# Where an identity matrix is made: GpSimd's select, or a running sum and a block transpose on VectorE

## The chip, the core and the metric

One core of a Trainium2 chip runs one program from the first load to the last store. The metric is the device time of that program in microseconds (us), lower is better. TensorE multiplies matrices, VectorE (DVE in the profile) and ScalarE (ACT) work element by element, GpSimd (POOL) makes constants, reduces over partitions and issues indirect transfers, and SyncE (SP) issues most of the loads.

## The reference

Linear attention, a mixture of experts over its output, and a gated feed-forward stage. Only the attention's beginning matters here:

```python
def phi(x):
    proj = np.einsum('bhsd,df->bhsf', x, w_phi)
    proj = proj - np.max(np.abs(proj), axis=-1, keepdims=True)
    return np.concatenate([np.exp(proj), np.exp(-proj)], axis=-1)
q_p, k_p = (phi(q), phi(k))
kv = np.einsum('bhsf,bhsd->bhfd', k_p, v)
z = np.sum(k_p, axis=2)
num = np.einsum('bhsf,bhfd->bhsd', q_p, kv)
den = np.einsum('bhsf,bhf->bhs', q_p, z)[..., None] + 1e-06
```

There are 4 batches of 8 heads, 576 tokens and 64 dimensions, and 128 features. The result, 2304 tokens of 512, goes through 8 experts (each token through one) and then through a feed-forward stage of width 768.

## The kernel before

The attention is cut into steps: on the k side a head quad of a 256-token unit (`k_T` transposes the keys, `k_proj` projects them, `k_acc` accumulates keys times values and the sums of the keys, `k_fin` ends a batch), on the q side a half batch and a head pair (`q_T` transposes, `q_front` projects and reduces over partitions on GpSimd, `q_sub`, `q_exp`, `q_num`, `q_den` and so on). Python generators, interleaved by `merge`, write the order of TensorE, SP, GpSimd and VectorE out by hand: each engine takes its instructions in that order. ScalarE is left to the scheduler. The first instructions of TensorE are eleven products that nothing uses (line 151), then `k_T(0)`, `k_T(1)`, `k_proj(0, 0)`, `k_proj(0, 1)` (twelve products), then the first query transposes `q_T(0, 0)`, `k_proj(1, 0)` and the first accumulation, `k_acc`.

Every transpose on TensorE is a product with the identity `ident`, a 128x128 tile in float32. `make_identity` (line 1154) makes it on GpSimd: a memset to zero and a select that writes ones where row and column are equal. It is called ahead of the block in which the order is written out. `Routing.__init__` (lines 573 to 601) then makes the constants of the routing on GpSimd (four iotas, several memsets, a select), and the attention makes its own (`ones`, two `zp`, `enp`, lines 157 to 165) after them in GpSimd's order. The routing's constants are used when the attention is over; `ones` in the sums of the keys. GpSimd's first work after the constants is the partition reduction of line 332.

Loads: SP issues the first key unit in two halves, its values, the first query block, and the next unit of keys and values (lines 91 and 108); ScalarE's queue issues the two copies of the projection weights into `w2` (lines 138 and 140). VectorE clears `wkH` and `wkL` (line 148; the unused products read `wkL`) and, when the weights are there, splits them (lines 152 to 156).

Of the kernel before, what the change touches and what calls it, by code (L numbers as in the profile page):

```python
# [18 lines left out]

#: steps of a batch's k side, of the first q work over two a unit, and of a batch's q side  # L20
PACE = 47, 9, 35


def merge(*streams):
    """Interleave streams of work; each is a list of (generator, its expected steps), and stages keep pace."""
    live = [[list(st), 0, 0] for st in streams]

    def progress(s):
        return s[1] + min(s[2] / s[0][0][1], 0.999)

    while live:
        for s in sorted(live, key=progress):
            try:
                if next(s[0][0][0]) == "blocked":
                    continue
                s[2] += 1
            except StopIteration:
                s[0].pop(0)
                s[1] += 1
                s[2] = 0  # L40
                if not s[0]:
                    live.remove(s)
            break
        else:
            raise RuntimeError("all streams blocked")


def rsqrt(nc, pool, out, in_, shape, nm):
    """out = in_ ** -0.5 by Newton steps from the exponent trick; yields between them."""
    g = pool.tile(shape, F32, tag=f"rs_g{nm}", name=f"rs_g{nm}")  # L50
    t = pool.tile(shape, F32, tag=f"rs_t{nm}", name=f"rs_t{nm}")
    i = pool.tile(shape, I32, tag=f"rs_i{nm}", name=f"rs_i{nm}")
    nc.vector.tensor_scalar(g, in_, 1e-30, None, op0=ALU.max)
    nc.vector.tensor_scalar(i, g.bitcast(I32), 1, None, op0=ALU.logical_shift_right)
    nc.vector.tensor_scalar(out.bitcast(I32), i, -1, 0x5F3759DF, op0=ALU.mult, op1=ALU.add)
    for _ in range(3):
        nc.vector.tensor_tensor(t, out, out, op=ALU.mult)
        nc.vector.tensor_tensor(t, t, g, op=ALU.mult)
        nc.vector.tensor_scalar(t, t, -0.5, 1.5, op0=ALU.mult, op1=ALU.add)
        nc.vector.tensor_tensor(out, out, t, op=ALU.mult)  # L60
        yield


def attention(tc, q, k, v, w_phi, expert_emb, tau, x_d, lraw, ssq, ident, io, late, rt):
# [11 lines left out]
    with ExitStack() as ctx:  # L76
# [6 lines left out]

        # ---- loads
        kt, vt, qt = {}, {}, {}
# [27 lines left out]

        # steps on the k side: a head quad of a 256-token unit, or the rests of two batches
        steps, pcs, loads = [], [], []
# [48 lines left out]
        enp = cp.tile([P, NP_, 32], F32, tag="enp", name="enp")  # L164
        nc.gpsimd.memset(enp, 0.0)

        def prep_experts():
# [27 lines left out]

        # ---- k side
        kT, kp, kvs, acc = {}, {}, {}, {}
# [100 lines left out]

        # ---- q side: unit u = (half batch, head pair)
        stk, pq, mq, ex, ot, dn = {}, {}, {}, {}, {}, {}  # L300
# [84 lines left out]
        def x_log(ts):  # L385
            """logits of a few tiles; and one over their denominators"""
            n = len(ts)
# [35 lines left out]

        # ---- order of work
        load_kv(2)
# [54 lines left out]
        def q_ahead(u):  # L480
            """front work that precedes back unit u - LEAD"""
            m, p = divmod(u, NP_)
            if u < NU:
                q_front(u)
            if u - 2 >= 0 and u - 2 < NU:
                q_sub(u - 2)
# [72 lines left out]

#: moves a double's exponent, in its upper word read as float32, to float32's bias  # L560
REBIAS = 2.0 ** -112
#: added and taken away, it rounds to a whole number
ROUND = 1.5 * 2.0 ** 23


#: products that keep the tensor engine's clock up where it waits: for the routing (four places), for the first loads
WARM = 8, 22, 8, 2, 11


class Routing:  # L570
    """Sort the tokens by expert: into blocks of 128 slots, each of one expert, and densely."""

    def __init__(self, tc, gp, rp, NT, E, NB):
        self.tc, self.nc, self.gp, self.rp = tc, tc.nc, gp, rp
        self.NT, self.E, self.NB = NT, E, NB
        nc, P = tc.nc, 128

# [28 lines left out]
    def one_hots(self, pool, r, nm, groups):  # L606
        """rows r (1 to 128) of the tiles' tokens as one-hot matrices, a group of tiles at a time"""
        P = 128
# [9 lines left out]
    def warm(self, bank, n):  # L618
        """products that nothing uses"""
        if n:  # L620
# [4 lines left out]
    def argmax(self, lraw, t0, t1):  # L625
        """one-hot expert of tiles t0 to t1 - 1; the first of equal logits wins"""
        V, P, E = self.nc.vector, 128, self.E
# [11 lines left out]
    def blocks(self, bank):  # L639
        """slot of every token, token of every slot, expert of every block; yields where the vector engine waits"""  # L640
        nc, gp, rp, P, NT, E, NB = self.nc, self.gp, self.rp, 128, self.NT, self.E, self.NB
# [11 lines left out]
        yield  # L653
        # slots of every expert's blocks, one block at least
        nb = t_([P, E], "nb")
# [9 lines left out]
        V.tensor_tensor(ohb, ohb.bitcast(F32), self.tid.unsqueeze(2).to_broadcast(full), op=ALU.mult)  # L665
        # token of every slot
        ps3 = bank("rt_tok")
        for group in self.one_hots(rp, rf, "R", (6, 6, 6)):
# [4 lines left out]
            yield  # L673
        # expert of every block
        eb = t_([1, NB, E], "eb")
# [5 lines left out]
        V.tensor_copy(self.s2t, ps3[:, 0:NB])  # L681
        # places of the experts in the dense order
        self.before = self.tmp(gp, [P, E], "before")
# [13 lines left out]
    def places(self, rp, gp, first, before, nm):  # L697
        """place of every token, from 0, less (P - 1) / 2; its expert's places start at `first`"""
        V, P, E, NT = self.nc.vector, 128, self.E, self.NT
# [10 lines left out]
    def rows(self, rp, pos, nm):  # L710
        """of places less (P - 1) / 2: row in the tile, from 1, and first place of the tile"""
        V, P, NT = self.nc.vector, 128, self.NT
# [6 lines left out]
    def dense(self, rp, bank, gate):  # L719
        """token, slot and gate of every place in the dense order"""  # L720
        nc, gp, P, NT, E = self.nc, self.gp, 128, self.NT, self.E
# [42 lines left out]
def gates(tc, rp, lraw, ssq, gate):  # L764
    """softmax weight of the chosen expert, token by token"""
    nc = tc.nc
# [22 lines left out]
class Experts:  # L789
    """Raw expert weights on chip: four chunks of [128, 2048], expert 0's first, reloaded when the expert changes."""  # L790

# [4 lines left out]
    def alloc(self, pool):  # L796
        """in the space of the attention's inputs, which are used up"""
        self.raw = [pool.tile([128, 2048], F32, tag=tag, name=f"raw{i}") for i, tag in enumerate(("kv", "kv", "q", "q"))]
        for i in range(4):
            self.load(i, slice(0, 1))  # L800
# [11 lines left out]
class Moe:  # L812
    """y = relu(x @ w1) @ w2, block by block of 128 slots"""

# [8 lines left out]
    def run(self, j0, j1, before=None, during=None):  # L823
        """blocks j0 to j1 - 1"""
        nc, sp, pp, wp, ex, ident = self.nc, self.sp, self.pp, self.wp, self.ex, self.ident
# [131 lines left out]
class Moe2:  # L957
    """h = max(y @ w1, y @ w2, y @ w3), out = h @ w_out, over thirds of the tokens"""

# [39 lines left out]
    def rebias(self, n):  # L999
        """double words: the exponent as float32 has it, still three bits too low"""  # L1000
        if n < 2 * self.NF and self.wide:
# [4 lines left out]
    def cut(self, n):  # L1006
        """a chunk of weights in float32: double words are cut to 24 bits; yields between steps"""
        if n >= 2 * self.NF:
# [30 lines left out]
    def gather(self, t):  # L1039
        """a tile of the dense order; its slots lie in the first t + 8 blocks"""  # L1040
        if t >= self.NT:
# [23 lines left out]
    def run(self, n0):  # L1065
        """all but the first third's y and the first n0 parts of the weights, which are there"""
        tc, nc, P, NF, NK, DM, G, TG, NT = self.tc, self.nc, self.P, self.NF, self.NK, self.DM, self.G, self.TG, self.NT
# [72 lines left out]
def tile_kernel(ctx, tc, q, k, v, w_phi, expert_emb, tau, w1, w2, m2_w1, m2_w2, m2_w3, m2_w_out, out):  # L1140
# [12 lines left out]
    ident = gp.tile([P, P], F32, tag="ident", name="ident")  # L1153
    make_identity(nc, ident)
    lraw = gp.tile([P, NT, E], F32, tag="lraw", name="lraw")
# [4 lines left out]
    with ExitStack() as rctx:  # L1160
        rp = rctx.enter_context(tc.tile_pool(name="rt", bufs=1))
        with tc.manual_schedule(engines={ET.PE, ET.SP, ET.Pool, ET.DVE}):
            rt = Routing(tc, gp, rp, NT, E, NB)
            attention(tc, q, k, v, w_phi, expert_emb, tau, x_d, lraw, ssq, ident, ew, lambda: ex.alloc(ew), rt)
    with tc.manual_schedule():
        pre = ctx.enter_context(tc.tile_pool(name="m2pre", bufs=1))
        m2 = Moe2(tc, pre, m2_w1, m2_w2, m2_w3, m2_w_out, NTOK, NB, ys, rt, out, ident)
        with mctx:
# [15 lines left out]
            def weights():  # L1184
                """the first parts of the next stage's weights"""
                m2.load_w(0)
# [73 lines left out]
```

## Time and profile before

| | us |
|---|---|
| median of 3 runs | 854.7 |
| the runs | 856.23, 852.54, 854.70 |
| span of the profiled execution | 855.8 |
| TensorE busy | 826.1 (97%) |
| VectorE busy | 548.4 (64%) |
| ScalarE busy | 493.2 (58%) |
| GpSimd busy | 162.0 (19%) |

The page gives no other time of the profiled execution than its span, from its first instruction to its last. Busy times are of that one execution. A matmul's end is modelled, so a busy TensorE is not one at its peak.

### The profile page before, as it was taken

Reading aid. Unit: us, or ns where it says so; the run is one execution under the profiler, and the core shown is the slowest. Engines: PE = TensorE matmul, PEld = TensorE weight load, DVE = VectorE, ACT = ScalarE, POOL = GpSimd, SP = SyncE. Lnnn points to the kernel's source line nnn. Section 1 sums busy time; section 2 is a strip of 40 time slices with the busy share of each in tenths; the row PEclk is TensorE's granted clock in tenths of the full one; section 3 lists DMA queues with packets and bytes.
Section 4 is the critical chain, followed back from the end, with each engine's and each line's share of the span. In section 5 each row is a group of like instructions: output and inputs, shape, how many; then the busy total and the mean of one; then the engine's idle time right before and its main releaser. Section 6 shows DMA issues by size and latency. Waiting matters only on the chain. (4 is left out here: it accounts for less than half of the span.)

```text
span 855.8 us, 13159 instructions
## 1 busy us (share of the span) xinstructions
PE 826.1 (97%) x5049; PEld 671.4 (78%) x5049; DVE 548.4 (64%) x705; ACT 493.2 (58%) x680; POOL 162.0 (19%) x116
## 2 busy tenths in 40 slices
PE   5989999999988999999999999999999999999996
PEld 4555565555567888888888888899989999899995
DVE  4886777767587999999889898788412222122210
ACT  3788868878647888888888796444221111211111
POOL 1234323233313122101051212000031001200001
PEclk9999999999998999999999999999999999999998
DMA  8331333310622435743644644344021000200001
GB/s 182 78 78 28 103 75 103 102 39 19 229 72 89 167 117 182 282 182 118 234 168 144 218 171 169 118 155 141 13 79 58 1 1 24 75 13 1 1 21 53
DMA packets 59649, 87.73 MB, mean 103 GB/s; under 512 B 7160, under 2 KB 37496, under 8 KB 59584
## 3 DMA queue, kind: packets, MB, share of 16 engines
q1 hardware_dynamic: 51376, 65.03, 23.8%
q0 software_dynamic: 4880, 15.99, 5.7%
q10 hardware_dynamic: 3328, 5.83, 1.8%
q8 instruction: 41, 0.67, 0.3%
q14 instruction: 24, 0.20, 0.1%
HBM read 129.58 MB, written 15.99 MB: 170 GB/s over the span
## 5 line engine op out<-in xcount | busy, mean ns | idle before, releaser
L864 DVE TENSOR_TENSOR wL<-raw,wH 128x2048 fp32r<-128x2048 f32 x88 | 199.6, 2287 | 18.3 <-ACT wH L863 17.9
L863 ACT CAST wH<-raw 128x2048 fp32r<-128x2048 f32 x88 | 167.6, 1915 | 30.8 <-PE ph L890 13.7
L1091 PE MATMUL ps<-yH,m2WH 128*128 128x384 f32 x432 | 146.1, 338 | 1.3 <-ACTq L1227 1.3
L1091 PE MATMUL ps<-yH,m2WL 128*128 128x384 f32 x432 | 146.0, 338 | 0.0
L1091 PE MATMUL ps<-yL,m2WH 128*128 128x384 f32 x432 | 146.0, 338 | 0.0
L332 POOL PARTITION_ALL_REDUCE mq<-pq x32 | 68.9, 2159 | 143.7 <-DVE pq L336 94.1
L1099 ACT CAST h2H<-mm 128x384 fp32r<-128x384 f32 x36 | 18.5, 513 | 118.4 <-DVE mm L1096 118.4
L1091 PEld LDWEIGHTS ps<-yH,m2WH 128*128 128x128 f32 x432 | 81.1, 188 | 1.8 <-ACTq L1227 1.7
L1091 PEld LDWEIGHTS ps<-yL,m2WH 128*128 128x128 f32 x432 | 81.1, 188 | 0.1
L1091 PEld LDWEIGHTS ps<-yH,m2WL 128*128 128x128 f32 x432 | 81.1, 188 | 0.0
L834 POOL DMA_INDIRECT xs<-x_d,s2t x22 | 43.7, 1988 | 155.5 <-PE psxT L873 93.6
L1045 POOL DMA_INDIRECT yg<-ys,c2s x18 | 26.2, 1454 | 245.4 <-PE psyT L1060 220.6
L922 PE MATMUL py<-wH,hH 128*128 128x512 f32 x176 | 70.4, 400 | 0.4 <-ACT hH L908 0.4
L922 PE MATMUL py<-wH,hL 128*128 128x512 f32 x176 | 69.1, 392 | 0.0
L922 PE MATMUL py<-wL,hH 128*128 128x512 f32 x176 | 68.7, 390 | 0.0
L1095 DVE TENSOR_TENSOR mm<-mm,ps 128x384 f32<-128x384 f32 x36 | 19.9, 552 | 76.2 <-PE ps L1091 76.2
L321 DVE TENSOR_TENSOR st<-psqT,st 64x288 fp32r<-64x288 f32 x64 | 44.7, 698 | 36.6 <-ACT st L317 34.6
L890 PE MATMUL ph<-wH,xH 128*128 128x512 f32 x176 | 57.4, 407 | 0.7 <-ACT xH L876 0.7
L890 PE MATMUL ph<-wL,xH 128*128 128x512 f32 x176 | 55.4, 396 | 0.0
L890 PE MATMUL ph<-wH,xL 128*128 128x512 f32 x176 | 55.2, 395 | 0.0
L1096 DVE TENSOR_TENSOR mm<-mm,ps 128x384 f32<-128x384 f32 x36 | 19.9, 554 | 45.6 <-PE ps L1091 45.6
L1113 ACT ACTIVATE ot<-pso,gatec 128x512 f32<-128x512 f32 x18 | 12.4, 688 | 60.3 <-PE pso L1111 33.0
(222 smaller groups left out, 1594.8 us busy)
## 6 DMA issues: line engine op xcount, KB each, us to landing
raw<-in_moe_w_dram SPq DMA_DIRECT2D x88, 1024.0 KB
wr<-in_moe_w_dram SPq DMA_DIRECT2D x18, 512.0 KB
ys<-y ACTq DMA_DIRECT2D x22, 256.0 KB
q<-in_q_dram SPq DMA_DIRECT2D x8, 576.0 KB
x_d<-x SPq DMA_DIRECT2D x18, 256.0 KB
kv<-in_v_dram SPq DMA_DIRECT2D x8, 512.0 KB
kv<-in_k_dram SPq DMA_DIRECT2D x7, 512.0 KB
wr<-in_moe_w_out_dram SPq DMA_DIRECT2D x6, 512.0 KB
```

Of the source, the lines that this page charges most:

```text
L321: nc.vector.tensor_tensor(st[o, :, :, 2 * rp + j], psv[x], st[x, :, :, 2 * rp + j].bitcast(F32), op=ALU.subtract)
L332: nc.gpsimd.partition_all_reduce(mx.rearrange("p a b -> p (a b)"), d.rearrange("p a b -> p (a b)"), P, ReduceOp.absmax)
L834: nc.gpsimd.indirect_dma_start(out=d, out_offset=None, in_=self.x_d, in_offset=bass.IndirectOffsetOnAxis(ap=self.s2t[:, j:j + 1], axis=0))
L863: nc.scalar.copy(wH, ex.raw[i])
L864: nc.vector.tensor_tensor(wL, ex.raw[i], wH.bitcast(F32), op=ALU.subtract)
L890: nc.tensor.matmul(ph[:, n * 512:(n + 1) * 512], a[:, cs], w[:, c * DF + n * 512:c * DF + (n + 1) * 512], start=(kc == 0 and f == 0), stop ...
L922: nc.tensor.matmul(py, a[:, cs], w[:, ws], start=(fc == 0 and q == 0), stop=(fc == 7 and q == 2))
L1045: self.nc.gpsimd.indirect_dma_start(out=d, out_offset=None, in_=self.ys[0:rows, :], in_offset=bass.IndirectOffsetOnAxis(ap=self.rt.c2s[:, ...
L1091: nc.tensor.matmul(ps, w[:, c], y[:, k], start=(k == 0 and q == 0), stop=(k == NK - 1 and q == 2))
L1095: nc.vector.tensor_tensor(m, m, pss[1], op=ALU.max)
L1096: nc.vector.tensor_tensor(m, m, pss[2], op=ALU.max)
L1099: nc.scalar.copy(hH[:, f], m)
```

## The change

`make_identity` goes. A new function makes the identity on VectorE: a row of ones is summed up, so that each of 32 columns holds its number from 1 to 32 in all partitions; the 32x32 blocks of that are transposed, so that each partition holds its own number within its group of 32; and for each of the four groups the columns are compared with that number, which writes ones and zeros into the diagonal blocks of a cleared `ident`. It is called as the first thing in the block whose order is written out, ahead of `Routing` and of the attention. The scratch tile's pool closes at the function's end. `Routing`'s constants move from its constructor into a method `prep`, which the attention calls after `enp`: GpSimd now has the attention's constants first and the routing's after them. The rest of the diff takes comments away.

```diff
-from concourse.masks import make_identity
...
+def identity(tc, out):
+
+    V = tc.nc.vector
+    with tc.tile_pool(name="idn", bufs=1) as pool:
+        a = pool.tile([128, 3, 32], F32, tag="idn", name="idn")
+        V.memset(a[:, 0], 1.0)
+        V.memset(out, 0.0)
+        V.tensor_tensor_scan(a[:, 1], a[:, 0], a[:, 0], 0.0, op0=ALU.mult, op1=ALU.add)
+        V.transpose(a[:, 2], a[:, 1])
+        for i in range(0, 128, 32):
+            V.tensor_scalar(out[i:i + 32, i:i + 32], a[i:i + 32, 1], a[i:i + 32, 2, 0:1], None, op0=ALU.is_equal)
+
...
         enp = cp.tile([P, NP_, 32], F32, tag="enp", name="enp")
         nc.gpsimd.memset(enp, 0.0)
+        rt.prep()
...
         self.NT, self.E, self.NB = NT, E, NB
+
+    def prep(self):
+        tc, gp, NT, E, NB = self.tc, self.gp, self.NT, self.E, self.NB
         nc, P = tc.nc, 128
...
     ident = gp.tile([P, P], F32, tag="ident", name="ident")
-    make_identity(nc, ident)
...
         with tc.manual_schedule(engines={ET.PE, ET.SP, ET.Pool, ET.DVE}):
+            identity(tc, ident)
             rt = Routing(tc, gp, rp, NT, E, NB)
```

## Rows read from the trace of the kernel before

**Rows 1.** The page: busy tenths of TensorE and its granted clock, 40 slices.

```profile
PE   5989999999988999999999999999999999999996
...
PEclk9999999999998999999999999999999999999998
```

**Rows 2.** TensorE's waits over the span: us in total, times, longest us.

```profile
PE pskT L210 <- POOL ident masks.py:199: 5.8, 1, 5.8
```

**Rows 3.** Timeline to 25 us: start us, us, engine, line, operation, tiles [idle before <-releaser].

```profile
0.82 0.56 ACTq L138 DMA_DIRECT2D w<-in_w_phi_dram  x1
...
1.22 0.27 DVE L148 MEMSET wkL<- 128x256 f32 x1
...
1.54 2.71 PE L151 MATMUL warm<-wkL 128*128 128x256 f32 x11 [1.54 <-DVE wkL L148]
...
5.28 0.23 DVE L152 CAST wqH<-w 128x128 fp32r<-128x128 f32 x1 [3.79 <-DMA w<-in_w_phi_dram]
...
6.46 0.23 DVE L156 CAST wkL<-wqL 64x128 fp32r<-64x128 f32 x1
...
9.62 0.14 POOL L580 IOTA we<- 128x8 f32 x1 [8.59 <-issue]
9.72 0.28 POOL masks.py:199 TENSOR_SCALAR_AFFINE_SELECT ident<-ident 128x128 f32<-128x128 f32 x1
...
10.06 1.97 PE L210 MATMUL pskT<-ident,kv 128*128 128x128 f32 x8 [5.80 <-POOL ident masks.py:199]
...
11.85 0.58 PE L227 MATMUL pskp<-wkH,kH 128*128 128x256 f32 x1
...
12.47 0.20 POOL L165 MEMSET enp<- 128x128 f32 x1
...
12.57 0.58 PE L227 MATMUL pskp<-wkH,kL 128*128 128x256 f32 x1
...
14.87 0.54 PE L312 MATMUL psqT<-ident,q 72*128 72x72 f32 x4
...
16.80 0.63 ACT L234 ACTIVATE kp<-pk 128x512 f32<-128x512 f32 x1
...
18.01 0.65 PE L260 MATMUL kv<-kp,kv 128*64 128x256 f32 x4 [1.85 <-ACT kp L235]
```

**Rows 4.** Pool configurations of lines 580 and 332: ns min/median/max, first and last start.

```profile
L580 POOLq MODIFY_POOL_CONFIG  x2: 8/8/8, 1.0 to 1.1; - x2
...
L332 POOLq MODIFY_POOL_CONFIG  x2: 11/11/11, 12.9 to 12.9; - x2
```

**Rows 5.** Stretches: busy us per engine, granted clock, DMA share, GB/s (last column).

```profile
0.00:9.00 9.00, 2.71 (x11) 2.42 (x11) 1.86 (x8) 1.28 (x1) 0.41 (x5) 1.00 0.78 193
9.00:11.40 2.40, 1.34 (x7) 1.35 (x8) 0.00 (x0) 0.19 (x1) 1.65 (x11) 1.00 1.21 192
11.40:13.90 2.50, 2.50 (x11) 2.06 (x11) 1.45 (x3) 0.98 (x2) 1.28 (x7) 1.00 1.18 227
```

**Rows 6.** Small VectorE operations by shape, count | busy us, mean ns | idle before.

```profile
L647 DVE TENSOR_TENSOR_SCAN inc<-d,oh 128x144 f32<-128x144 f32 x1 | 0.5, 457 | 0.0
...
L394 DVE TENSOR_SCALAR r<-psxd 128x24 f32<-128x24 f32 x2 | 0.4, 183 | 1.3 <-PE psxd L391 1.3
...
L659 DVE TENSOR_TENSOR_SCAN cb<-o,nb 128x8 f32<-128x8 f32 x1 | 0.2, 175 | 0.0
```

**Rows 7.** Two later stretches: length, busy us of PE, PEld, DVE, ACT, POOL, granted clock.

```profile
18.00:25.30 7.30, 7.29 (x36) 4.65 (x37) 5.46 (x9) 5.32 (x9) 0.00 (x0) 0.54 0.24 53
...
30.00:60.00 30.00, 26.85 (x223) 15.79 (x220) 28.68 (x58) 26.85 (x51) 11.86 (x6) 0.99 0.36 91
```

**Rows 8.** Timeline, 25 to 45 us: the first partition reduction, the next query transposes.

```profile
28.91 2.16 POOL L332 PARTITION_ALL_REDUCE mq<-pq  x1 [16.23 <-ACT pq L330]
...
29.43 0.42 PE L312 MATMUL psqT<-ident,q 72*128 72x72 f32 x4
```

## The prediction, made before the change was run

> **What bounds the kernel now.** I read the forty slices of the page first. TensorE is busy nearly everywhere except in the first slice, and no granted clock is far below full for a whole slice [rows 1]. So the change, which touches only constants made at the very start, can win time in that first slice or nowhere. Next comes the list of waits of TensorE over the whole run: its largest single wait is 5.8 us, and what ended it is the identity made on GpSimd [rows 2]. Third, the timeline of the first 20 us shows how that comes about. GpSimd's first iota starts at 9.62 and the select that writes the ones of `ident` at 9.72, after 8.59 us in which it waited for nothing that the profile lists [rows 3]. The rows of line 580 tell what lies there: a pool configuration is issued at 1.1 [rows 4]. I read the 8.5 us from 1.1 to 9.62 as the price of that configuration. TensorE, done with its unused warm products at 4.25, stands still until 10.06, then transposes keys, and everything behind it (copy on ScalarE, difference on VectorE, projection at 11.85, query transposes at 14.87, exponentials at 16.80, first accumulation at 18.01) hangs on that start [rows 3].
>
> [...]
>
> **The change, part by part.**
>
> *Removed from the path: identity behind the pool configuration.* The identity no longer needs GpSimd. With it ready, the first key transposes have to wait for the warm products and for the first key transfer, half of a 512 KB unit and the first thing in SP's queue. That whole unit and the two loads of the weights are 0.59 MB, reached at 3.1 us by the mean rate of the first 9 us [rows 5], so the transfer is not what they wait for.
>
> *Added: eight instructions on VectorE, ahead of the two clears and the warm products.* Two memsets: I take for each the 0.27 us of a 256 column one [rows 3], which is more than these 32 and 128 columns need. A running sum of 32 elements: 0.175 us with 8 and 0.457 with 144 elements [rows 6], so 0.23 in between. The block transpose has no row; its bounds are a 24 column operation (0.183) and that 144 element scan (0.457) [rows 6], and I take 0.23, nearer to the row of its own width. Four comparisons of 32x32: 0.183 each by the 24 column row [rows 6]; the six casts and differences from 5.28 to 6.69 [rows 3] start 0.235 apart on average though each works on at most 128 columns, so I take 0.235. Sum: 0.54 + 0.23 + 0.23 + 0.94 = 1.9 us, with ends of 1.4 (eight at 0.175) and 2.6 (the wide scan for scan and transpose, and 0.29 a comparison).
>
> [...]
>
> Queued behind these eight on VectorE are the clears of `wkH` and `wkL`; behind these, on TensorE, the eleven warm products, and behind them the key transposes. The products thus start at 1.54 + 1.9 = 3.4 and last 2.71, to 6.15 [rows 3]; ends 5.65 and 6.85. The first key transposes start there instead of at 10.06: 3.9 us earlier (3.2 to 4.4). The split weights are ready at 6.69 [rows 3], which is before the projection wants them (11.85 - 3.9 = 7.95), so the later clears cost nothing else.
>
> *What is late next: the queries.* TensorE takes its work in order, and after the twelve projections come the transposes of the first query block, at 14.87 now, at 10.95 with the shift. Their 576 KB transfer lies fourth in SP's queue. Up to its end the queues carry 256 + 256 + 512 + 576 KB from SP and 64 KB of weights, 1.70 MB. By the rates of the first stretches, 1.74 MB had moved by 9.0 us; with the next key unit 2.23 MB, reached at 11.5; with the next values too 2.75 MB, reached at 13.9 [rows 5]. The transfers share the DMA engines, so the query block lands between 8.9 and 13.9. I let it end with the unit behind it and add some tenths for the hand-over: 11.8, an estimate. Then its transposes start at 11.9 instead of 14.87, 3.0 us earlier, and ScalarE, which has the copies of these transposes ahead of the first exponentials (16.80) in its order, passes this shift on to the accumulation, 18.01 to 15.0 [rows 3]. So 0.9 of the 3.9 us is lost again, and it is also the cover for the identity: up to 0.9 us more on VectorE would cost nothing.
>
> *Moved: GpSimd's order.* `ones`, the two `zp` and `enp` now come before the iotas. All of GpSimd's constants together took from 9.62 to 12.67 [rows 3], so the moved ones end by 3.9 at the latest, and are ready long before the first sums use them. The iotas and the rest then follow behind the configuration, at 3.9 + 8.5 = 12.4 or earlier, and end by 15.5. Their users (routing, far behind) cost nothing. Behind them comes a second configuration, for the partition reduction, now issued at 12.9 [rows 4]; with another 8.5 us the engine would be ready at 24.0 at the latest. The first reduction is wanted at 28.91 now [rows 8], at 25.9 with the shift. So 1.9 us of cover remain at the least. The next query block, transposed at 29.43 now [rows 8], is issued behind the first key and value units as before and has been loaded by then.
>
> *A possible new wait.* The scratch tile of the identity lives in a pool that closes before the attention's constants are placed, so the first of these, `w2`, may get the same bytes. Then its two loads on ScalarE's queue, issued at once today, wait for the last comparison, at 0.94 + 1.9 = 2.85. From the issue of these loads to the use of the weights passed 5.28 - 0.82 = 4.5 us [rows 3]; then they would come at 7.3, be split by 8.7, and the differences of the keys, which VectorE does behind that, by 9.4; the products that need these start at 12.57 now [rows 3]. That is a shift of 3.2, about that of the queries. I count it at nothing, with ends of nothing and of the fourth case below.
>
> *Sum.* 5.8 us of waiting removed; 1.9 us given to VectorE's chain ahead of the warm products; 0.9 us given to the query transfer: 3.0 us gained. On the profiled execution's span of 855.8 that makes 852.8; this span lies 1.1 us above the median of the runs shown, 854.7, and from the median it makes 851.7.
>
> **The rivals.**
> *The shift is larger.* If the queries land at 8.9, the transposes pass without a wait and 3.9 us remain. The granted clock can add to that: the stretch from 18 to 25.3 ran at 0.54 with TensorE busy 7.29 of 7.3 us, while VectorE had 5.46 of work in it [rows 7]. With TensorE busy from 3.4 on without the long pause, the clock may be up there; VectorE then bounds the stretch, worth up to 1.8. Against it: TensorE still pauses for the queries and for the first exponentials (1.85 us before 18.01 [rows 3]), and after this pattern the clock fell. Time: 854.7 - 3.9 to 5.7, 849.0 to 850.8, say 850.0.
> *Another wait takes most of it.* The queries land with the next values at 13.9, or the weights come a microsecond or two later than above. Gain 0.9, time 853.8.
> *Slower: the weights fall behind SP's queue.* If `w2` waits for the scratch tile and its loads are then served only with the 2.75 MB that SP has queued, they land at 13.9; with 1.4 for the splits and 0.7 for the difference of the keys, the products that need it start at 16.1 instead of 12.57 [rows 3]: 3.5 us late, 858.2. It decides from a landing later than 10.4. Against it: today the loads, issued side by side with SP's, were used at 5.28, when less than half of that had moved.
> *The change does nothing:* not if the select leaves GpSimd; then the 5.8 us row must go.
>
> **How the numbers follow.** Forecast, gain of 2 to 4 us: 0.55. Larger shift: 0.22. Most of it lost: 0.17. Slower: 0.06. About 0.5% (4.3 us) is what a measurement of this kernel can tell from no change, so faster means below 850.4, slower above 859.0. Most of the larger shift lies below 850.4, with a little of the forecast's edge: faster 0.22. Of the slower case half may pass 859.0: slower 0.03. Same: 0.75. The range takes in the larger shift's middle and the lost gain: 849.2 to 855.0.
>
> **What would show it.** In the changed kernel's timeline: eight VectorE instructions ending near 2.8, warm products from 3.4, key transposes near 6.2 with no wait on GpSimd; TensorE then waiting for a DMA of `q`, the query transposes near 11.9, the first accumulation near 15.0, the first partition reduction near 26. I am wrong if `w2` is used later than 8, if the reduction's configuration is waited for, if the query transposes pass without a wait, or if the 3 us seen at 15 are no longer there at 60.

## The result, and the profile after

| | before | after |
|---|---|---|
| median time, us | 854.69 (852.54 to 856.23) | 859.13 (857.33 to 860.73) |
| ratio after/before, 95% | | 1.0057 [1.0046, 1.0069] |
| profiled execution: time, span, us | -, 855.8 | 857.33, 855.6 |
| mean granted clock of that execution | 0.987 | 0.985 |

The change made the kernel 4.4 us slower; 851.7 with a range to 855.0 had been forecast. The profiled executions don't show it: both spans are about 855.7. The time of the profiled execution after lies 1.7 us above its span. With as much around it, the one before (855.8) took about 857.5, more than any of its six timed runs. So the kernel before was profiled once more, as `e0_before_again`; that execution (853.56 us, span 851.8) lies 0.9 us below the median of its set, as the one after lies 1.8 below its own, and what follows is compared with it. One timed run of the experiments below (1021.92 us at a mean granted clock of 0.751, of `e3_order_only`) was in a slow state and is left out.

The page of the kernel after, busy tenths of TensorE and granted clock in 40 slices, beside [rows 1]:

```profile
PE   5899999999979999999999999999999999999996
...
PEclk8899999999998999999999999999999999999998
```

The first slice is no fuller than before, the second is emptier, and the clock dropped in both. The timeline of the kernel after, to 28 us (columns as in [rows 3]):

```profile
0.90 0.09 DVE L52 MEMSET idn<- 128x32 f32 x1 [0.90 <-PEq L1260]
...
1.04 0.20 DVE L54 TENSOR_TENSOR_SCAN idn<-idn 128x32 f32<-128x32 f32 x1
1.27 0.21 DVE L55 STREAM_TRANSPOSE idn<-idn 128x32 f32<-128x32 f32 x1
1.52 0.97 DVE L57 TENSOR_SCALAR ident<-idn 32x32 f32<-32x32 f32 x4
...
2.53 0.56 ACTq L150 DMA_DIRECT2D w<-in_w_phi_dram  x1
...
5.72 1.85 PE L223 MATMUL pskT<-ident,kv 128*128 128x128 f32 x8
...
10.91 0.23 DVE L164 CAST wqH<-w 128x128 fp32r<-128x128 f32 x1 [7.75 <-DMA w<-in_w_phi_dram]
...
11.98 0.55 PE L240 MATMUL pskp<-wkH,kH 128*128 128x256 f32 x1 [4.41 <-DVE wkH L168]
...
14.52 0.14 POOL L596 IOTA we<- 128x8 f32 x1 [10.79 <-issue]
...
18.71 0.65 PE L273 MATMUL kv<-kp,kv 128*64 128x256 f32 x4 [1.25 <-ACT kp L248]
...
27.44 2.16 POOL L345 PARTITION_ALL_REDUCE mq<-pq  x1 [11.25 <-ACT pq L343]
```

The wait for the identity is gone: the key transposes start at 5.72 instead of 10.06. But the load of the weights on ScalarE's queue is issued at 2.53 instead of 0.82, when the last comparison has ended, and the weights are used at 10.91 instead of 5.28. TensorE waits 4.41 us for them, and the first projection starts at 11.98 (11.85 before), the first accumulation at 18.71 (18.01). A second loss follows later. ScalarE, from 26 to 37 us, kernel after:

```profile
26.60 0.70 ACT L343 COPY pq<-psqf 128x288 f32<-128x288 f32 x2
29.52 0.63 ACT L247 ACTIVATE kp<-pk 128x512 f32<-128x512 f32 x1 [2.22 <-DVE pk L245]
30.06 0.61 ACT L248 ACTIVATE kp<-pk 128x512 f32<-128x512 f32 x1
30.78 0.63 ACT L247 ACTIVATE kp<-pk 128x512 f32<-128x512 f32 x1
31.32 0.61 ACT L248 ACTIVATE kp<-pk 128x512 f32<-128x512 f32 x1
31.84 1.33 ACT L330 CAST st<-psqT 64x288 fp32r<-64x288 f32 x2
33.19 0.58 ACT L226 CAST kH<-pskT 128x512 fp32r<-128x512 f32 x1
33.67 0.62 ACT L189 ACTIVATE esq_junk<-emb 8x512 f32<-8x512 f32 x1
```

And the same work of the kernel before, in `e0_before_again`:

```profile
26.21 0.70 ACT L330 COPY pq<-psqf 128x288 f32<-128x288 f32 x2
26.79 0.63 ACT L176 ACTIVATE esq_junk<-emb 8x512 f32<-8x512 f32 x1
...
27.70 1.38 ACT L317 CAST st<-psqT 64x288 fp32r<-64x288 f32 x2 [0.20 <-PE psqT L312]
29.13 0.63 ACT L234 ACTIVATE kp<-pk 128x512 f32<-128x512 f32 x1
29.67 0.61 ACT L235 ACTIVATE kp<-pk 128x512 f32<-128x512 f32 x1
30.31 0.58 ACT L213 CAST kH<-pskT 128x512 fp32r<-128x512 f32 x1
```

ScalarE does the same instructions in another order. Before, the square of `emb` and the two copies of the query transposes (`st`) come ahead of the exponentials (`kp`); after, they come behind four of them, and ScalarE stands 2.22 us for VectorE's `pk` (what the exponentials read: projections less their maxima) with those copies queued behind. VectorE, which wants `st` next, then stands too, in the kernel after:

```profile
33.20 1.34 DVE L334 TENSOR_TENSOR st<-psqT,st 64x288 fp32r<-64x288 f32 x2 [2.45 <-ACT st L330]
```

Stretch 30 to 33 us, columns as in [rows 7], first after, then `e0_before_again`:

```profile
30.00:33.00 3.00, 2.31 (x26) 0.84 (x24) 0.71 (x2) 2.88 (x6) 0.00 (x0) 1.00 0.21 55
```

```profile
30.00:33.00 3.00, 3.00 (x31) 1.53 (x30) 2.82 (x8) 2.98 (x7) 0.37 (x1) 1.00 0.23 58
```

VectorE did 0.71 us of work in these 3 us against 2.82. The diff doesn't touch ScalarE's program. The orders of TensorE, VectorE, GpSimd and SyncE are written out by hand in this kernel; ScalarE's is left to the scheduler. What it plans from, no run shows. Compared instruction by instruction, the two kernels' ScalarE orders differ in 25 places, all from the 22nd to the 72nd instruction.

### The profile page after: what moved, and what is told of

Its sections match the earlier page's. It is cut to its first block, busy times and chain, and to the rows that moved or that the text cites. A ratio compares the mean times of both kernels' runs of the same rounds, so it can differ in the third digit from the quotient of the medians.

```text
span 855.6 us, 13166 instructions
## 1 busy us (share of the span) xinstructions
PE 825.3 (96%) x5049; PEld 670.7 (78%) x5049; DVE 549.5 (64%) x713; ACT 492.8 (58%) x680; POOL 161.0 (19%) x114
## 5 line engine op out<-in xcount | busy, mean ns | idle before, releaser
L330 ACT CAST st<-psqT 64x288 fp32r<-64x288 f32 x64 | 43.6, 682 | 8.4 <-PE psqT L325 7.9
```

What stands on the lines that cost most here:

```text
L330: nc.scalar.copy(st[x, :, :, 2 * rp + j], psv[x])
```

## The experiments

The first theory had one cause: the scratch tile `idn` shares its bytes with `w2`, so the loads of the weights are held. The rival was the moved order on GpSimd; a third theory, ScalarE's order, was formed when the first had fallen. Each run's median is set beside that of the kernel before in the same set. A convenient clock within one execution is the row of the partition reductions on GpSimd (they recur 32 times): they show at which point a kernel falls behind.

**The kernel before, once more** (`e0_before_again`). No edit.

> The kernel before once more, as it is, for a second profile. The profile of before had a span of 855.8 us while its six timed runs have a median of 854.7; the six runs of the changed kernel lie 1.7 us above their spans. If a profile is one draw of a time that scatters with where TensorE's clock falls (clock theory), this one has its low-clock stretches elsewhere, up to 20 us apart, and a span that differs by 1 to 4 us, most likely near 853. If the start is a fixed cost (loads theory), the first accumulation starts at 18.0 again, the span is 855.8 again and the low clock lies at 18.5 to 25.4 again.

Measured: 854.47 against 854.5, 1.0004 [0.9989, 1.0018]; span 851.8. First, second and ninth reduction:

```profile
27.04 2.16 POOL L332 PARTITION_ALL_REDUCE mq<-pq  x1 [14.83 <-ACT pq L330]
32.63 2.14 POOL L332 PARTITION_ALL_REDUCE mq<-pq  x1 [3.43 <-ACT pq L330]
...
69.03 2.14 POOL L332 PARTITION_ALL_REDUCE mq<-pq  x1 [1.47 <-DVE pq L336]
```

The first came at 28.91 in the execution profiled first [rows 8], so two executions of one kernel can stand 1.9 us apart there; the span is 4.0 us shorter, at the end of what the clock theory gave. From the ninth on, every profiled kernel here keeps its distance from this one within 0.4 us until the 32nd, at 219 us: in the attention, what the start decides is decided by 70 us.

**The scratch tile kept** (`e1_scratch_kept`), in a pool that stays open, so that the loads are not held.

```diff
-    with tc.tile_pool(name="idn", bufs=1) as pool:
-        a = pool.tile([128, 3, 32], F32, tag="idn", name="idn")
+    a = pool.tile([128, 3, 32], F32, tag="idn", name="idn")
...
-            identity(tc, ident)
+            identity(tc, ident, rp)
```

> The changed kernel, but the scratch tile of the identity lies in a pool that stays open through the attention, so that the loads of the weights wait for nothing. Loads theory (the loads of the weights are held by the scratch tile, go out behind SP's and are used at 10.9 instead of 5.3): the weights are used near 5.3 again, projections start near 7.5, query transposes near 11.9, first accumulation near 15.0, and the time falls to 850.5 to 852.5, 7 us below the changed kernel. Clock theory (the 4.4 us come from where TensorE's clock falls later, after whatever start): the start improves as said, but the time stays at 855 or above. Third theory (GpSimd's second configuration, which now comes later, is what costs): the first partition reduction starts not before 26, and the time is 854 to 857.

Measured: 856.18 against 854.5, 1.0013 [1.0001, 1.0025]. About 2.7 us of the loss are repaired, and the start runs nearly as forecast (first projection product at 7.58, 3.8 us ahead of `e0_before_again`), yet no gain is left. First and second reduction:

```profile
26.06 2.16 POOL L344 PARTITION_ALL_REDUCE mq<-pq  x1 [12.46 <-ACT pq L342]
33.71 2.15 POOL L344 PARTITION_ALL_REDUCE mq<-pq  x1 [5.49 <-ACT pq L342]
```

It is 1.0 us ahead of the kernel before at the first reduction and 1.1 behind at the second. The theory of one cause fell. The second pool configuration doesn't explain the time either: the first reduction waits for ScalarE's `pq`. ScalarE's order here turned out to be that of the kernel after in all but four places, not that of the one before.

**The loads held, alone** (`e2_held_loads_only`): the kernel before with a second identity, made as in the change and not used.

```diff
+            identity(tc, rp.tile([P, P], F32, tag="ident2", name="ident2"))
```

> The kernel before (identity by GpSimd's select, order of its constants as before), with the changed kernel's eight instructions on VectorE made into a second identity that nobody uses, and their scratch tile in a pool that closes as in the change; so the loads of the weights are held, and nothing else of the change is there. Loads theory: the weights are used at 10.5 to 11, the identity is there at 10.0, first accumulation near 18.7, and the time is that of the changed kernel, 858 to 860. Clock theory: also a late start, but without the changed kernel's early burst of transposes; if that burst is what matters the time is 855 to 856.

Measured: 856.47 against 854.5, 1.0023 [1.0013, 1.0033], 2.0 us slower, between the ranges of the two theories. With the identity still coming from GpSimd, the held loads cost this much by themselves:

```profile
2.53 0.56 ACTq L151 DMA_DIRECT2D w<-in_w_phi_dram  x1
...
9.90 1.97 PE L223 MATMUL pskT<-ident,kv 128*128 128x128 f32 x8 [3.97 <-POOL ident masks.py:199]
11.02 0.36 DVE L165 CAST wqH<-w 128x128 fp32r<-128x128 f32 x1 [7.86 <-DMA w<-in_w_phi_dram]
...
13.79 0.58 PE L240 MATMUL pskp<-wkH,kL 128*128 128x256 f32 x1
```

Its ninth reduction, at 71.04, is 2.0 behind.

**GpSimd's order, alone** (`e3_order_only`): the kernel before with the attention's constants ahead of the iotas; the select of `ident` stays on GpSimd.

```diff
         nc.gpsimd.memset(enp, 0.0)
+        rt.prep()
```

> The kernel before with only GpSimd's order changed: the attention's constants first, the routing's after them. In this order the pool configuration stands ahead of the select that finishes the identity, behind three memsets. All theories: identity 0.7 to 1.5 us later, at 10.7 to 11.5, first accumulation at 18.7 to 19.5. If the start is a fixed shift the time is 855.4 to 856.2; if the clock's place matters more, it can come out up to 4 us off that on either side.

Measured: 855.3 against 854.5, 1.0013 [0.9999, 1.0026]. The constants put ahead delay the select, which starts at 10.49 against 9.26; after the change no select is there to be delayed. So nothing of the 4.4 us is seen to come from the moved order; the next run, which contains it, is not above the kernel before. ScalarE's order is that of the kernel before in this run and in the one with the loads held alone.

**The scratch tile kept and ScalarE's order of the kernel before** (`e4_kept_old_order`). Edges between neighbours on one engine fix the order; in the trace all 680 ScalarE instructions stand as in the kernel before.

```diff
+        act = [i for i in nc.cur_bb.bb.instructions if i.engine == mybir.EngineType.Activation]
+        order = [24, 30, 27, 28, 21, 22, 29, 25, 26, ...]
+        for a, b in zip(order, order[1:]):
+            tc.add_manual_dep(act[b], act[a].name, ..., reason="order")
```

> As the run with the kept scratch tile, but ScalarE's order, which the scheduler plans and which came out otherwise in the changed kernel from its 22nd instruction to its 72nd, is held to that of the kernel before (edges between successive ScalarE instructions, no waits). Order theory (the scheduler, believing in an earlier start, put other exponentials ahead, and on the chip ScalarE, VectorE and TensorE stand still for 2 to 3 us near 30 us for it): that stall is gone, the 3 us of the earlier start reach the end, and the time is 850.5 to 852.0. Clock theory (the low clock after 34 us comes of the earlier start itself): the stall near 30 is gone or not, the clock still falls between 30 and 62 us, and the time stays at 854.5 to 856.5.

Measured: 853.39 against 854.35, 0.9995 [0.9981, 1.0009]: both losses are gone, and no gain is told from nothing. The time lies between the ranges of the two theories. The stall is gone, and this is nearly the start that had been forecast, with the first and second reduction:

```profile
5.38 0.23 DVE L163 CAST wqH<-w 128x128 fp32r<-128x128 f32 x1 [2.10 <-DMA w<-in_w_phi_dram]
...
5.85 1.91 PE L222 MATMUL pskT<-ident,kv 128*128 128x128 f32 x8
...
12.19 0.71 PE L324 MATMUL psqT<-ident,q 72*128 72x72 f32 x4 [2.46 <-DMA q<-in_q_dram]
...
15.51 1.12 PE L272 MATMUL kv<-kp,kv 128*64 128x256 f32 x4 [1.24 <-ACT kp L247]
```

```profile
26.09 2.16 POOL L344 PARTITION_ALL_REDUCE mq<-pq  x1 [13.01 <-ACT pq L342]
31.96 2.14 POOL L344 PARTITION_ALL_REDUCE mq<-pq  x1 [3.71 <-ACT pq L342]
```

TensorE waits for the queries until 12.19 (forecast 11.9) and accumulates from 15.51 (forecast 15.0). That is 2.5 us ahead of [rows 3], but 1.85 ahead of `e0_before_again` (17.36), and 0.7 ahead of it at the second reduction.

**ScalarE's order of the kernel after, alone** (`e5_before_new_order`), in the kernel before: the same edges with the other order.

> The kernel before with nothing changed but ScalarE's order, which is held to that of the changed kernel for the 72 instructions in which they differ. Order theory: start as before (first accumulation near 18), then a stall of 2 to 3 us between 28 and 36 us that the kernel before does not have, the clock falling after it, and a time of 856.5 to 858.5, 2 to 4 us above the kernel before. Clock theory (the start's pattern of work decides): 854 to 855, as the kernel before.

Measured: 857.26 against 854.35, 1.0030 [1.0017, 1.0044]. First and second reduction:

```profile
28.48 2.16 POOL L332 PARTITION_ALL_REDUCE mq<-pq  x1 [15.79 <-ACT pq L330]
...
36.17 2.14 POOL L332 PARTITION_ALL_REDUCE mq<-pq  x1 [5.52 <-ACT pq L330]
```

With no other change, this order costs 2.6 us by the ratio, 2.9 by the medians. From the first reduction to the second pass 7.6 to 7.7 us in the three profiled kernels with the new order (after, 27.44 to 35.05; `e1_scratch_kept`; and this one), and 5.6 to 5.9 in every one with the old.

**The change with ScalarE's order of the kernel before** (`e6_after_old_order`): the held loads stay.

> The changed kernel as it is, with the loads of the weights held, and only ScalarE's order held to that of the kernel before. Order theory: 855.5 to 857, the 2 to 4 us of the order are gone and what is left over the kernel before is the held loads alone (856.5 in the run that had nothing but these). Clock theory: 858.5 to 860, as the changed kernel.

Measured: 856.3 against 854.35, 1.0015 [1.0004, 1.0026]: the change without its second loss. The identity's gain less the held loads leaves 1.3 to 2.0 us of loss.

**TensorE kept busy** (`e7_kept_old_order_busy`, `e8_before_busy`). The kernel with the scratch tile kept and the old ScalarE order held throughout, with 18 products that nobody uses ahead of the first query transposes and 14 ahead of the first accumulation; and the kernel before with 16 ahead of its first accumulation.

```diff
+        def keep(n):
+            ps = bank("keep")
+            for _ in range(n):
+                nc.tensor.matmul(ps[:, 0:2 * NF], wkL[:, 0:NF], wkL, start=True, stop=True)
```

> The run with the kept scratch tile and ScalarE's old order, with products that nothing uses put into TensorE's two pauses at the start: 18 ahead of the first query transposes (it waited 2.5 us there for the queries) and 14 ahead of the first accumulation (1.2 us). That run gained 3 us until 13 us and kept only 1, with the granted clock at half from 11.4 to 21.6 us. If those pauses are why the clock fell, it stays up from about 8 us on, TensorE no longer bounds 15 to 22 us, and the time falls by 1 to 2 us more, to 851.5 to 852.5. If the loss has another cause (VectorE and ScalarE are the bound there anyway), the clock stays up and the time stays at 853 to 854. If the products themselves are in the way, 854 or more.

> The kernel before, ScalarE's order held as it is, with 16 such products ahead of the first accumulation alone, where TensorE stood still for 1.85 us before the clock fell to half at 18 us. If the pause is why it fell, the clock is up from 15 us on without a break until the routing, and the time is 1 to 2 us below the kernel before: 852.5 to 853.5. Otherwise 854 to 855.

Measured: 853.59 against 855.18, 0.9984 [0.9969, 1.0000], and 854.77 against 855.18, 1.0000 [0.9986, 1.0014]. Stretch 17.6 to 21.6 us of `e4_kept_old_order`, `e7_kept_old_order_busy`, `e0_before_again` and `e8_before_busy`, in this order (granted clock third from the end):

```profile
17.60:21.60 4.00, 4.00 (x20) 2.76 (x20) 2.79 (x5) 2.96 (x6) 0.00 (x0) 0.50 0.53 131
```

```profile
17.60:21.60 4.00, 4.00 (x42) 2.30 (x40) 3.35 (x5) 3.92 (x7) 0.00 (x0) 1.00 0.74 168
```

```profile
17.60:21.60 4.00, 4.00 (x22) 2.52 (x19) 2.61 (x4) 3.24 (x6) 0.00 (x0) 0.57 0.78 176
```

```profile
17.60:21.60 4.00, 4.00 (x37) 2.70 (x34) 3.11 (x5) 3.83 (x8) 0.00 (x0) 1.00 0.69 158
```

TensorE was busy for all of the 4 us in each; at a granted clock of 1.00 it ran 42 and 37 matmuls where it ran 20 and 22 at 0.50 and 0.57. First accumulation and first reduction of `e7_kept_old_order_busy`, then of `e8_before_busy`:

```profile
15.69 0.65 PE L272 MATMUL kv<-kp,kv 128*64 128x256 f32 x4 [0.22 <-ACT kp L247]
...
24.43 2.16 POOL L344 PARTITION_ALL_REDUCE mq<-pq  x1 [11.24 <-ACT pq L342]
```

```profile
17.20 0.65 PE L260 MATMUL kv<-kp,kv 128*64 128x256 f32 x4
...
25.91 2.16 POOL L332 PARTITION_ALL_REDUCE mq<-pq  x1 [13.82 <-ACT pq L330]
```

With the clock at 1.00 in both, the 1.5 us between their accumulations are still 1.5 at the first reduction, and the forecast's gain is nearly all there: 24.43 against the 27.04 of `e0_before_again`, and still 2.6 us ahead at the third. Then the execution of the first fell to a mean clock of 0.58 from 54 to 58 us and was 1.2 ahead at the ninth. In the kernel before, the busy TensorE put the ninth reduction 1.1 us earlier, at 67.93.

The medians don't follow. Both lie where the expectations put them if the pauses were not the cause (853 to 854, 854 to 855), although the profiled executions stood at 1.00 from 11.4 to 21.6 us. So it is shown at the start of single executions, and not in the time, that the pauses cost clock (0.50 and 0.57 from 17.6 to 21.6 us with them, 1.00 with the products). Part of it is seen in the traces: in these two executions TensorE waits 1.1 us for ScalarE's `h` near 489 us, behind a wait of ScalarE of 1.9 us for an expert's weights at 476 us, and no other profiled execution has that wait of TensorE. Their spans, 852.8 and 852.3, end up above the 851.8 of `e0_before_again`. Whether the timed runs lose it there too is open.

The first of the two has the lowest ratio of all, 1.4 us (0.16%) below the kernel before, at the edge of what its interval tells from nothing; from `e4_kept_old_order` its interval doesn't tell it.

## Why the prediction was wrong

**What added up.** Against the kernel before, by medians: held loads +2.0 us (run alone), ScalarE's new order +2.9 (run alone), the earlier identity without either -1.0, which its interval doesn't tell from nothing. The sum is +3.9, measured was +4.4. Beside the held loads the earlier identity shows no gain: `e6_after_old_order`, which has both, lies 2.0 above the kernel before, as the held loads alone do, and with the order's 2.9 that makes 4.9. The forecast had only the third term, and had it at -3.0.

**The step "A possible new wait".** The mechanism was named and priced at nothing; here it failed. The hold was as worked out: issue at 2.53 (2.85 forecast). The length from issue to use was taken as today's 4.5 us, giving 7.3; it was 8.4, giving 10.91. That 4.5 had been measured on loads issued beside SP's first. Held until 2.53, they came when the transfer engines were full (a busy share of 0.99 from 2.5 to 5.3 us). Stretches of the kernel after, columns as in [rows 5]:

```profile
2.50:5.30 2.80, 2.09 (x10) 2.09 (x10) 0.54 (x2) 1.28 (x1) 1.18 (x4) 1.00 0.99 280
5.30:10.90 5.60, 2.28 (x11) 1.93 (x10) 0.00 (x0) 1.17 (x2) 0.00 (x0) 0.99 1.13 222
```

From the issue to the use 2.0 MB moved (0.78 from 2.5 to 5.3, 1.24 behind that); with the loads free, in `e1_scratch_kept`, 0.9 MB from the start to the use at 5.31 (5.3 us at 170 GB/s). The small loads were served among SP's large ones. Their 160 packets are alone on their queue, `q10`. Its row for 2.6 to 4.5 us of `e0_before_again`, then for 5.2 to 9.8 us of the kernel after (packets, MB, share of 16 engines):

```profile
q10 hardware_dynamic: 160, 0.07, 13.0%
```

```profile
q10 hardware_dynamic: 160, 0.07, 7.8%
```

All 160 lie in these 1.9 and 4.6 us, beside 0.49 and 1.00 MB of SP's queue. The latency scatters, too: in the three profiled executions with held loads the weights were used at 10.91, 11.02 and 12.66 (`e6_after_old_order`), in the eight others at 5.16 to 5.68. The fourth case of the forecast was this one, with a landing of 13.9, a threshold of 10.4 and a chance of 0.06. The use at 10.91 lies past the threshold, and the cost (2.0 alone, 2.9 between `e6_after_old_order` and `e4_kept_old_order`) within its 3.5. The argument against it ("used at 5.28, when less than half of that had moved") spoke only of loads issued first.

**The gain carried to the end.** The sum takes the 3.0 us of the start off the time of the whole kernel, with no term for what comes behind it. This failed twice. First, ScalarE's order was taken as given. It is planned, and the plan moved with the identity: it is the old one where the loads are held alone or GpSimd's constants moved alone, and the new one where the identity comes from VectorE, with the loads held or, but for four places, free. The new one takes 2.0 us between the first two reductions of the profiled executions (7.6 against 5.6), whatever had been won before. Nothing in the diff or in [rows 2 to 7] could show it; that ScalarE alone has no written order could have been read in the kernel, and would have been a rival. Second, the clock. [rows 7] showed TensorE busy without a break from 18 to 25 us at 0.54, and the forecast carries its gain whole through this stretch. But the clock there was not the same under both starts: with the earlier identity TensorE paused 2.5 us for the queries and stood at 0.50 from 11.4 to 21.6 (`e4_kept_old_order`), where the kernel before stood at 1.00 from 11.4 to 17.6 (`e0_before_again`); with the unused products it was 1.00 from 11.4 to 21.6 in both kernels. The 1.85 us by which the accumulation of `e4_kept_old_order` was ahead of `e0_before_again` (15.51 against 17.36) had shrunk to 0.95 by the first reduction. With unused products in the pauses the lead was 2.6 there; in the time that gain is not seen. The rival "larger shift" hoped for this without the pause, and saw the pause that spoke against it; that the low clock would take from the forecast itself was not priced.

**What held.** The chain on VectorE ended at 2.49, 1.6 us after it began (1.9 forecast; the ends were 1.4 and 2.6). The four comparisons took 0.24 us each (0.235 forecast), the 128x32 float32 transpose 0.21 (0.23 forecast). The key transposes came at 5.72 (6.15 forecast, ends 5.65 and 6.85), without a wait for their transfer. That transfer had been put at 3.1 us by the mean rate of 9 us, which is no rate of the start: from 0 to 2.5 us only 26 GB/s moved in the kernel after. The queries, once the loads were free, were waited for until 12.19 (11.9 forecast). The second pool configuration stayed covered: the first reduction, at 27.44, waited for ScalarE's `pq` and not for GpSimd.

**The range and the base.** The range, 849.2 to 855.0, left out both losses, and slower by over 0.5% had a chance of 0.03: half of the one case in which the loads come late, and nothing for a planned order. The profiled execution was said to lie 1.1 us above the median by its span; with the 1.7 us around the span it was 2.8. The forecast was counted from the median, so the number didn't suffer, but the rows came from an unusually slow draw. The term for the queries was too small even against these rows: the lead of `e4_kept_old_order` was 4.2 us at the key transposes (5.85 against 10.06) and 2.5 at the accumulation, so 1.7 us went there and not 0.9. Against `e0_before_again` the lead at the accumulation was 1.85, where 3.0 had been forecast.

## What to carry to other kernels

A scratch tile in a pool that closes is not free (2.0 us here): look which tile gets its bytes next, what fills that tile, and what traffic that transfer now falls in; a latency read from a transfer that was first in line is no price for one that comes late (4.5 us against 8.4 here). When a change moves the start of an engine with a written order, compare the order of every engine that is left to the scheduler, instruction by instruction, before believing a gain: here that order alone was worth nearly three microseconds. And an earlier start before a wait that stays only lengthens the pause; in the profiled executions here TensorE's clock charged for it (0.50 against 1.00 from 14 to 17.6 us, in `e4_kept_old_order` and `e0_before_again`).

## What the runs showed of the hardware

The gap behind GpSimd's pool configuration is not constant. Its first iota came 8.5 us after the configuration in the kernel before [rows 3, 4], and 10.7 us in the kernel after (3.8 to 14.52, nothing between that the profile lists). In ten profiled executions it is the longer the later the configuration is issued: 7.9 to 8.6 us in the five with the issue near 1.1, 9.3 to 9.8 in the three near 2.1, 10.6 and 10.7 in the two near 3.8. Why is open.

The granted clock differs between executions of one kernel. `e0_before_again` stood at 1.00 from 54 to 66 us, the execution of the same kernel that was profiled first at a mean of 0.86; their distance grew from 2.2 us at the sixth reduction to 3.6 at the eighth. The profiled execution of `e5_before_new_order` stood at 0.59 from 62 to 66 and went from 3.6 us behind at the third reduction to 5.6 at the ninth. What sets off such a stretch near 60 us in one execution and not in another was not settled.
